# Strassen's scheme for the first product of batches 1 to 3 in an attention-and-FFN kernel, with a hand-written program order

## The chip, the cores and the metric

The kernel runs on one core of one Trainium2 chip. The metric is the device time of one execution in microseconds (us); below it is shown beside the span that the profiler recorded, which runs from the first to the last instruction. Engines are called by the profile's names: PE is TensorE's matmul and PEld its weight load, DVE is VectorE, ACT is ScalarE, POOL is GpSimd and SP issues the DMAs.

## The reference

For each of four batches, q, k and v are 6080 x 256. The columns of q and k are normalized, a 256 x 256 softmax is formed from them, and v is multiplied by it. The result goes through a two-layer network with an ELU in between.

```python
qn = q / (np.linalg.norm(q, axis=1, keepdims=True) + 1e-06)
kn = k / (np.linalg.norm(k, axis=1, keepdims=True) + 1e-06)
s = kn.transpose(0, 2, 1) @ qn / tau
a = softmax(s)                         # over the last axis, 256 x 256
x = (v @ a).reshape(24320, 256)
h = x @ w_in                           # 256 -> 2048
g = np.where(h > 0.0, h, np.exp(np.minimum(h, 0.0)) - 1.0)
out = g @ w_out                        # 2048 -> 256
```

## The kernel before

The softmax matrix is folded into the first weights: for each batch the kernel forms `wp` = a @ w_in (256 x 2048), so that h = v @ wp. Every large product runs in three matmuls instead of one: an operand is split into a part `hi` in the type fp32r and the remainder `lo`, and hi*hi, hi*lo and lo*hi are added up in PSUM (`split`, L113 to L115: a cast on ACT and a subtraction on DVE).

The 6080 positions of a batch are cut into 12 chunks of 512 or 496 columns (8 and 4 of them; `chunk_sizes`). One **step** is one chunk `c` and one block `f` of 128 of the 2048 hidden rows; there are 16 steps in a chunk and 768 in all. In a step, `h_item` (L417) runs six matmuls into a PSUM bank `ph` (two halves of 256 inputs, three terms each; L423 to L425). `elu` (L430) turns the bank into g: on even steps as ACT Exp (L438), DVE min and add (L439) and DVE max (L440), on odd steps as ACT Relu (L434), ACT Exp (L435) and one DVE instruction (L436). `split_g` (L443) casts g on ACT (L114) and takes the remainder on DVE (L115). Three steps later (`LAG`), `out_item` (L455) multiplies g by w_out, again with six matmuls (L461, L463, L465), into two banks that collect a chunk's output over 16 steps and are then copied by ACT (L487) and stored.

The order of the work is that of `take` (L833): step i emits the first product of step i, the split of step i-1 and the second product of step i-3. Beside it stand what the next batch needs, at step numbers that are written out in tables (`side`, `loose`, `fine`): loading q and k in 24 groups of rows, squaring them for the norms (L181, L182), splitting them and multiplying them into the Gram matrices (`gram_item`, L195; L203 and L210, 512 and 256 columns wide), then the norms and the softmax (L264 to L331), the transposes (L333), and `wp` itself (`wp_item`, L363). The matmuls of `fine` are threaded between those of `out_item`. Over batch 0's first four chunks the order on PE, DVE and ACT is the program's; from there on a scheduler places the instructions of the steps.

GpSimd does almost nothing: it clears a few tiles (L169). PSUM's eight banks are two for the Gram matrices, three for `ph` and what shares its tag `w`, and three for outputs (tag `o`).

## Time and profile before

| | |
|---|---|
| times of two runs | 2165.7 and 2166.98 us, median 2166.34 us |
| span of the profiled execution (no other time of it is given) | 2163.4 us |
| PE busy | 2158.6 us in 10240 recorded matmuls |
| DVE busy | 1527.0 us |
| ACT busy | 1469.1 us |
| POOL busy | 3.3 us in 11 instructions |
| DMA | 120.77 MB, 55 GB/s of HBM traffic over the span |

The time is the median of the runs without the profiler. The span is 2.9 us shorter than that median. Busy times are sums of recorded durations; the duration of an instruction on ACT or DVE runs until its result is written, and the next one may start a little earlier, so start times tell how densely instructions follow each other. A row of the timeline gives the start, the duration, the engine, the line, the operation, and the tiles with their shapes; in brackets stand an idle time ahead of it and what ended that.

### The profile page before, as it was taken

To read this page: it belongs to the slowest core of one execution; us is meant where nothing else is said; L and a number is where in the kernel's file an instruction comes from. 1 tells how busy PE (TensorE), PEld (TensorE's weight loads), DVE (VectorE), ACT (ScalarE), POOL (GpSimd) and SP (SyncE) were. 2 spreads that over 40 slices of the span, in tenths; PEclk is the share of its full clock that TensorE was granted. 3 is DMA by queue.
4 is the path that set the end of the run, shared out by engine and by line. 5 is a ranking of instruction groups with operands and counts; after the bars stand their busy time and mean duration, and the time that the engine had idled before them with its cause. 6 is when DMAs were issued, how large, how long until landed. Compare 5 with 4: busy or idle time off the path is not lost.

```text
span 2163.4 us, 27196 instructions
## 1 busy us (share of the span) xinstructions
PE 2158.6 (100%) x10240; PEld 1911.9 (88%) x10240; DVE 1527.0 (71%) x2358; ACT 1469.1 (68%) x2422; POOL 3.3 (0%) x11
## 2 busy tenths in 40 slices
PE   9999999999999999999999999999999999999999
PEld 8888888899888888889988888888998888888998
DVE  7987777778766776776776677667776666666665
ACT  6877777667666666666766666666776666666665
POOL 0000000000000000000000000000000000000000
PEclk9999999999999999999999999999999999999999
DMA  9320222221111111111111112111112000000000
GB/s 357 107 78 30 78 69 68 68 65 49 59 38 50 49 59 49 59 58 46 39 59 39 49 50 68 49 58 49 56 31 67 20 30 27 23 20 11 20 10 20
DMA packets 62532, 120.77 MB, mean 56 GB/s; under 512 B 6208, under 2 KB 16064, under 8 KB 62400
## 3 DMA queue, kind: packets, MB, share of 16 engines
q1 hardware_dynamic: 62256, 118.91, 16.6%
q8 instruction: 80, 1.31, 0.2%
q14 instruction: 52, 0.43, 0.1%
q10 hardware_dynamic: 144, 0.13, 0.0%
HBM read 92.01 MB, written 27.00 MB: 55 GB/s over the span
## 4 chain that ended last, share of the span: by engine, by line
PE 100%; ACT 0%; DVE 0%; issue 0%
PE po L465 15%; PE po L463 15%; PE ph L423 15%; PE po L461 15%; PE ph L424 15%; PE ph L425 15%; PE gram L203 3%; PE gram L549 2%; PE gram L210 1%; PE pw L374 1%; PE pw L373 1%; PE pw L375 1%; PE pe L549 0%; PE pw L370 0%; PE pd L222 0%; PE pt L337 0%
## 5 line engine op out<-in xcount | busy, mean ns | idle before, releaser
L114 ACT CAST g<-e 128x512 fp32r<-128x512 f32 (+1 forms) x768 | 469.6, 611 | 483.5 <-DVE e L440 281.6
L115 DVE TENSOR_TENSOR g<-e,g 128x512 fp32r<-128x512 f32 (+1 forms) x768 | 525.6, 685 | 323.0 <-ACT g L114 295.6
L465 PE MATMUL po<-g,wo 128*128 128x512 f32 (+1 forms) x1536 | 579.3, 377 | 0.0
L463 PE MATMUL po<-g,wo 128*128 128x512 f32 (+1 forms) x1536 | 579.2, 377 | 0.0
L461 PE MATMUL po<-g,wo 128*128 128x512 f32 (+1 forms) x1536 | 578.9, 377 | 0.0
L423 PE MATMUL ph<-vt,wp 128*128 128x512 f32 (+1 forms) x1472 | 555.4, 377 | 0.0
L425 PE MATMUL ph<-vt,wp 128*128 128x512 f32 (+1 forms) x1472 | 554.5, 377 | 0.0
L424 PE MATMUL ph<-vt,wp 128*128 128x512 f32 (+1 forms) x1472 | 554.5, 377 | 0.0
L436 DVE SCALAR_TENSOR_TENSOR e<-e,ph 128x512 f32<-128x512 f32 (+1 forms) x416 | 283.2, 681 | 242.5 <-ACT e L435 241.9
L434 ACT ACTIVATE e<-ph 128x512 f32<-128x512 f32 (+1 forms) x416 | 246.6, 593 | 129.1 <-PE ph L425 114.4
L461 PEld LDWEIGHTS po<-g,wo 128*128 128x128 f32 x1536 | 290.3, 189 | 37.9 <-DVE scr L478 0.2
L463 PEld LDWEIGHTS po<-g,wo 128*128 128x128 f32 x1536 | 290.3, 189 | 37.8
L465 PEld LDWEIGHTS po<-g,wo 128*128 128x128 f32 x1536 | 290.7, 189 | 34.8 <-DVE g L115 0.3
L424 PEld LDWEIGHTS ph<-vt,wp 128*128 128x128 f32 x1472 | 278.2, 189 | 36.2
L425 PEld LDWEIGHTS ph<-vt,wp 128*128 128x128 f32 x1472 | 278.2, 189 | 36.1
L423 PEld LDWEIGHTS ph<-vt,wp 128*128 128x128 f32 x1472 | 278.2, 189 | 36.1
L435 ACT ACTIVATE e<-e 128x512 f32<-128x512 f32 (+1 forms) x416 | 261.3, 628 | 12.6
L440 DVE TENSOR_TENSOR e<-ph,e 128x512 f32<-128x512 f32 (+1 forms) x352 | 240.6, 684 | 10.4
L438 ACT ACTIVATE e<-ph 128x512 f32<-128x512 f32 (+1 forms) x352 | 207.9, 591 | 31.1 <-PE ph L425 29.2
L439 DVE TENSOR_SCALAR e<-e 128x512 f32<-128x512 f32 (+1 forms) x352 | 147.0, 418 | 20.7 <-ACT e L438 20.6
L182 DVE TENSOR_TENSOR acc<-acc,sq 128x1024 f32<-128x1024 f32 x84 | 102.6, 1221 | 12.2 <-ACT sq L181 11.1
L203 PE MATMUL gram<-qk 128*128 128x512 f32 x268 | 101.6, 379 | 0.0
(134 smaller groups left out, 1183.1 us busy)
## 6 DMA issues: line engine op xcount, KB each, us to landing
raw<-in_q_dram SPq DMA_DIRECT2D x76, 256.0 KB, 2.7
raw<-in_k_dram SPq DMA_DIRECT2D x76, 256.0 KB, 3.0
v<-in_v_dram SPq DMA_DIRECT2D x32, 512.0 KB, 3.6
out_dram<-o SPq DMA_DIRECT2D x56, 256.0 KB, 2.1
v<-in_v_dram SPq DMA_DIRECT2D x16, 496.0 KB, 3.5
out_dram<-o SPq DMA_DIRECT2D x31, 248.0 KB, 2.1
wraw<-w_scr SPq DMA_DIRECT2D x12, 512.0 KB, 3.2
room<-in_q_dram SPq DMA_DIRECT2D x16, 256.0 KB, 5.2
```

The costliest lines, as they stand in the source:

```text
L114: nc.scalar.copy(hi, src)
L115: nc.vector.tensor_sub(lo, src, hi.bitcast(F32))
L423: nc.tensor.matmul(ph[:, 0:n], wp[kt][:, 0, fs], hi, start=(kt == 0), stop=False)
L424: nc.tensor.matmul(ph[:, 0:n], wp[kt][:, 0, fs], lo, start=False, stop=False)
L425: nc.tensor.matmul(ph[:, 0:n], wp[kt][:, 1, fs], hi, start=False, stop=(kt == KT - 1))
L434: nc.scalar.activation(ev, pv, AF.Relu, scale=-1.0)
L435: x = nc.scalar.activation(ev, ev, AF.Exp, scale=-1.0)
L436: y = nc.vector.scalar_tensor_tensor(ev, ev, -1.0, pv, op0=ALU.add, op1=ALU.max)
L440: y = nc.vector.tensor_tensor(ev, pv, ev, op=ALU.max)
L461: nc.tensor.matmul(o, wo[:, f, 0, ds], hi, start=first(c, f), stop=False)
L463: nc.tensor.matmul(o, wo[:, f, 1, ds], hi, start=False, stop=False)
L465: nc.tensor.matmul(o, wo[:, f, 0, ds], lo, start=False, stop=last(c, f))
```

## The change

Batch 0 stays as it was (some tiles share other buffers, and its first weights lie in another layout). From batch 1 on, a **unit** takes the place of four steps: one chunk `c` and one quarter `fq` (512) of the hidden rows. There are 144 units. In a unit, the 256 x 512 weights are cut into four blocks A11 to A22 (the first index names the half of the hidden rows, the second the half of the 256 inputs) and v's chunk into B11 to B22 (the second index names the half of the columns). Four sums of A-blocks (S1 to S4) and four of B-blocks (T1 to T4) are formed by GpSimd (`s_sum`, `t_sum`), split into hi and lo, and seven block products are made (`product`): A11 B11, S3 T3, S2 T2, A12 B21, S1 T1, S4 B22 and A22 T4. Each product is six matmuls of 256 (or 248) columns, so a unit has 42 of them; before, four steps had 24 of 512 (or 496) columns for the same h. The second product is as before, 24 matmuls to a unit (`multiply_out`).

Three PSUM banks hold the products. `bank_a` collects A11 B11 and A12 B21. `bank_b` is first filled by ACT with a copy of A11 B11, and then collects S2 T2, S1 T1 and S4 B22; ACT copies it out after the first (`u2`) and after the second (`u4`). `bank_e` collects S3 T3 and A22 T4; DVE adds it to `u4` after the first and to `u2` after the second. The four blocks of h are then `bank_a` (e11), `bank_b` at the end (e12), `u2` (e21) and `u4` (e22). All four go through Relu and Exp on ACT and one DVE instruction (`relu_exp`, `largest`). The cast to hi is made by DVE for e11 and e12 and by ACT for e22 and e21 (`hi_part`), the remainder by DVE (`lo_part`).

From the first unit on, the order on all engines is the program's. What the next batch and the next chunk need is put into lists with a cost for each task (`task`), and `spend` emits as many of them as a budget allows at fixed places of a unit: on ACT after the cast of e21 and after `u4`, on DVE ahead of `largest` of e11 and after the remainder of e11, on GpSimd in the same two places. `beside` threads the next batch's PE work between the second product's matmuls. GpSimd takes the sums, the casts of T and B blocks, and most of the additions of squares.

Three places of the new order matter below. In the rows, `s_0` to `s_3` are the tiles of A- and S-blocks, `t_0` and `t_1` those of T-blocks, `b_0` and `b_1` the two banks that units take in turn as `bank_b`, `held` is one tile that holds u2, e12 and e21, and `po` are the output banks.

The first is PE. One step of before (chunk 37, within batch 3):

```order
L423 MATMUL ph_14735<-vt_37_14461,wp_3_0_13661 128x512
L424 MATMUL ph_14735<-vt_37_14461,wp_3_0_13661 128x512
L425 MATMUL ph_14735<-vt_37_14461,wp_3_0_13661 128x512
L423 MATMUL ph_14735<-vt_37_14461,wp_3_1_13662 128x512
L424 MATMUL ph_14735<-vt_37_14461,wp_3_1_13662 128x512
L425 MATMUL ph_14735<-vt_37_14461,wp_3_1_13662 128x512
L461 MATMUL po_37_0_14667<-g_14706,wo_83 128x512
```

The start of a unit of the change (chunk 38, first quarter, batch 3):

```order
L1093 MATMUL bank_a_16953<-s_2_4967,s_0_4774 128x256 x6
L1093 MATMUL bank_e_16961<-t_0_4714,s_0_4774 128x256 x6
L1116 MATMUL po_37_0_16697<-g2_16844,wo_83 128x512
L1117 MATMUL po_37_0_16697<-g2_16844,wo_83 128x512
L1118 MATMUL po_37_0_16697<-g2_16844,wo_83 128x512
L1116 MATMUL po_37_1_16713<-g2_16844,wo_83 128x512
L1117 MATMUL po_37_1_16713<-g2_16844,wo_83 128x512
L1118 MATMUL po_37_1_16713<-g2_16844,wo_83 128x512
L1093 MATMUL b_0_5085<-t_0_4714,s_0_4774 128x256 x6
L1093 MATMUL bank_a_16953<-s_3_5093,s_0_4774 128x256 x6
L1116 MATMUL po_37_0_16697<-g1_16906,wo_83 128x512
```

Where a bank was filled once and read by the other engines, the banks are now read and filled again within the unit: the six matmuls into `b_0` (S2 T2) follow ACT's copy into that bank, and the six into `bank_a` (A12 B21) stand behind them on PE.

The second is ACT. Before, around the same place:

```order
L438 ACTIVATE e_14388<-ph_14381 128x512
L114 CAST g_14412<-e_14388 128x512
L434 ACTIVATE e_14408<-ph_14401 128x512
L435 ACTIVATE e_14408<-e_14408 128x512
L114 CAST g_14432<-e_14408 128x512
```

And ACT over the unit of the change, from the last two activations of the unit ahead (on e21) up to those on e21 of this one:

```order
L1176 ACTIVATE held_5089<-held_5089 128x512
L1455 COPY b_0_5085<-bank_a_16953 128x512
L1182 CAST g2_16943<-held_5089 128x2x256
L1468 COPY held_5089<-b_0_5085 128x512
L1175 ACTIVATE e_e11_5091<-bank_a_16953 128x512
L1176 ACTIVATE e_e11_5091<-e_e11_5091 128x512
L1476 COPY e_u4_5090<-b_0_5085 128x512
L1175 ACTIVATE e_e22_5092<-e_u4_5090 128x512
L1176 ACTIVATE e_e22_5092<-e_e22_5092 128x512
L1182 CAST g2_17038<-e_e22_5092 128x2x256
L1175 ACTIVATE held_5089<-b_0_5085 128x512
L1176 ACTIVATE held_5089<-held_5089 128x512
```

The copy that fills `b_0` for this unit (L1455) stands behind everything that ACT does for e22, e12 and e21 of the unit ahead, and three copies of PSUM banks (L1455, L1468, L1476) have come in.

The third is DVE over the same unit, from the remainders of the unit ahead to the remainder of e22:

```order
L1179 SCALAR_TENSOR_TENSOR held_5089<-held_5089 128x512
L1185 TENSOR_TENSOR g1_16906<-held_5089,g1_16906 128x2x256
L1185 TENSOR_TENSOR g2_16943<-held_5089,g2_16943 128x2x256
L1179 SCALAR_TENSOR_TENSOR e_e11_5091<-e_e11_5091,bank_a_16953 128x512
L1182 CAST g1_17003<-e_e11_5091 128x2x256
L1477 TENSOR_TENSOR e_u4_5090<-bank_e_16961,e_u4_5090 128x512
L1185 TENSOR_TENSOR g1_17003<-e_e11_5091,g1_17003 128x2x256
L1179 SCALAR_TENSOR_TENSOR e_e22_5092<-e_e22_5092,e_u4_5090 128x512
L1489 TENSOR_TENSOR held_5089<-bank_e_16961,held_5089 128x512
L1185 TENSOR_TENSOR g2_17038<-e_e22_5092,g2_17038 128x2x256
```

The addition that completes u4 (L1477), which ACT's work on e22 reads, stands behind DVE's work on e11 (L1179 and L1182).

The diff, cut to the new functions and the loop that sets the order:

```diff
--- before.py
+++ after.py
-    def split_g(c, e):
+    def split_g(c, e, i):
         n = span(c)[2]
-        g = work.tile([P, 2, CH], F32R, tag="g", bufs=4, name="g")
+        if i % 2 == 0:
+            state["g"] = work.tile([P, 2, 2, CH], F32R, tag="g", bufs=3, name="g")
+        g = state["g"][:, i % 2]
         split(g[:, 0, 0:n], g[:, 1, 0:n], e[:, 0:n])
         return g
...
@@ -746,7 +753,7 @@
     splits = [(1, 0, 0), (2, 4, 4), (3, 7, 9)]
-    splits += [(c, (c - 1) * FT + 9, (c - 1) * FT + 12) for c in range(M, NCH)]
+    splits += [(c, (c - 1) * FT + 9, (c - 1) * FT + 12) for c in range(M, NB)]
...
-    for b in range(1, B):
-        s0 = M * FT if b == 1 else chunk_of(b - 1) * FT + FT
...
+    HF = CH // 2
+    MATRICES = ("A11", "A22", "A12", "S1", "S2", "S3", "S4")
+    SPARE = len(MATRICES)
+
+    def new_s(fq):
+        s_tiles[fq] = work.tile([P, SPARE + 1, 2, HF], F32R, tag="wp", bufs=2 * KT, name=f"s_{fq}")
+
...
+    def s_scale(b, fq, ct):
+
+        if ct == 0:
+            new_x(b, fq)
+        pw = state.pop((b, "pw", fq, ct))
+        nc.scalar.activation(
+            x_of(b, fq, 2 * ct, 2 * ct + 2), halves_of_turns(pw), AF.Copy, scale=state[b, "rs"][:, ct : ct + 1]
+        )
+
+    def s_sum(b, fq, k):
+        a21, a11, a22, a12, s1, s2, s3, s4 = (x_of(b, fq, y, y + 1) for y in range(8))
+        add, sub = nc.gpsimd.tensor_add, nc.gpsimd.tensor_sub
+        (
+            lambda: add(s1, a21, a22),
+            lambda: sub(s2, s1, a11),
+            lambda: sub(s3, a11, a21),
+            lambda: sub(s4, a12, s2),
+        )[k]()
+
+    def s_hi(b, fq, lo, hi, copy=nc.scalar.copy):
+        copy(s_tiles[fq][:, lo:hi, 0], x_of(b, fq, 1 + lo, 1 + hi))
+
+    def s_lo(b, fq, lo, hi):
+        s = s_tiles[fq]
+        nc.vector.tensor_sub(s[:, lo:hi, 1], x_of(b, fq, 1 + lo, 1 + hi), s[:, lo:hi, 0].bitcast(F32))
+
+    s_tiles = {}
+    PARTS = ((0, 1), (1, 3), (3, 5), (5, SPARE))
+
+    b = 1
+    if True:
+        s0 = M * FT
         s1 = chunk_of(b) * FT
         length = s1 - FT - 14 - s0
...
@@ -860,8 +936,582 @@
     for i in range(M * FT + LAG):
         take(i)
     in_order.close()
-    for i in range(M * FT + LAG, len(steps) + LAG):
+
+
+    ACT, DVE, POOL, PE, SP, CAST, ADD = "act", "dve", "pool", "pe", "sp", "cast", "add"
+    queues = {(e, level): [] for e in (ACT, DVE, POOL, PE, SP, CAST, ADD) for level in range(4)}
+
...
+    def spend(engine, budget, now):
+        order = [(engine, 0), (engine, 1), *((x, y) for x in SHARED.get(engine, ()) for y in range(2)), (engine, 2), (engine, 3)]
+        for key in order:
+            queue = queues[key]
+            while queue and queue[0].ready(now, 0):
+                t = queue[0]
+                cost = t.cost if key[0] == engine else t.cost[engine]
+                if cost > budget:
+                    break
+                queue.pop(0)
+                budget -= cost
+                if key[0] == engine:
+                    t.fn()
+                else:
+                    t.fn({ACT: nc.scalar.copy, DVE: nc.vector, POOL: nc.gpsimd.tensor_copy if key[0] == CAST else nc.gpsimd}[engine])
+                t.done = now
+
...
+    PERIOD = 4
+    units = [(c, fq) for c in range(NB, NCH) for fq in range(FQ)]
+    begins = {c: PERIOD * FQ * (c - NB) for c in range(NB, NCH + 1)}
...
+    def t_sum(c, k):
+        hn = half_of(c)
+        if k == 0:
+            state["tt", c] = work.tile([P, 4, HF], F32, tag="raw", bufs=5, name=f"tt_{c}")
+        v = vraw[c]
+        b11, b12 = (v[:, 0, x * hn : (x + 1) * hn] for x in range(2))
+        b21, b22 = (v[:, 1, x * hn : (x + 1) * hn] for x in range(2))
+        t1, t3, t2, t4 = (state["tt", c][:, y, 0:hn] for y in range(4))
+        sub, add = nc.gpsimd.tensor_sub, nc.gpsimd.tensor_add
+        (
+            lambda: sub(t1, b12, b11),
+            lambda: sub(t3, b22, b12),
+            lambda: add(t2, t3, b11),
+            lambda: sub(t4, b21, t2),
+        )[k]()
+
+    def t_hi(c, k):
+        hn = half_of(c)
+        nc.gpsimd.tensor_copy(t_groups[c % 2][:, k : k + 2, 0, 0:hn], state["tt", c][:, k : k + 2, 0:hn])
+
+    def t_lo(c, k):
+        hn = half_of(c)
+        t = t_groups[c % 2][:, k : k + 2]
+        nc.vector.tensor_sub(t[:, :, 1, 0:hn], state["tt", c][:, k : k + 2, 0:hn], t[:, :, 0, 0:hn].bitcast(F32))
+        for y in range(2):
+            operands[c, TERMS[k + y]] = t[:, y]
+
+    TERMS = ("T1", "T3", "T2", "T4")
...
+    def b_hi(c, k):
+        to, src, hn, _ = block_of(c, k)
+        nc.gpsimd.tensor_copy(to[:, 0, 0:hn], src)
+
+    def b_lo(c, k):
+        to, src, hn, name = block_of(c, k)
+        nc.vector.tensor_sub(to[:, 1, 0:hn], src, to[:, 0, 0:hn].bitcast(F32))
+        operands[c, name] = to
...
+    def product(bank, c, fq, a, t, begin=False):
+        hn = half_of(c)
+        w, m = s_tiles[fq][:, MATRICES.index(a)], operands[c, t]
+        hi, lo = (in_turns(m[:, x, 0:hn]) for x in range(2))
+        for j in range(2):
+            js = slice(j * P, j * P + P)
+            for k, (x, y) in enumerate(((0, hi), (0, lo), (1, hi))):
+                nc.tensor.matmul(
+                    bank[:, j, 0:hn],
+                    w[:, x, js],
+                    y,
+                    start=(begin and j == 0 and k == 0),
+                    stop=(j == 1 and k == 2),
+                    skip_group_check=True,
+                )
...
+    def plan_chunk(c):
+
+        if c + 1 >= NCH:
+            return
+        d, t = c + 1, begins[c]
+        if c == NB:
+            task(SP, 0, lambda: new_t_group(d), when=t, level=0)
+        x = task(SP, 0, lambda: vraw.__setitem__(d, load_v(d)), when=t + PERIOD, level=0)
+        for k in range(4):
+            x = task(POOL, 0.65, lambda k=k: t_sum(d, k), [x], when=t + PERIOD, level=0)
+            if k % 2 == 1:
+                y = task(POOL, 0.65, lambda k=k: t_hi(d, k - 1), [x], when=t + PERIOD, level=0)
+                task(DVE, 0.685, lambda k=k: t_lo(d, k - 1), [y], when=t + PERIOD, level=0)
+        for k, when in enumerate((2 * PERIOD, 3 * PERIOD, 3 * PERIOD + 1)):
+            y = task(POOL, 0.35, lambda k=k: b_hi(d, k), [x], when=t + when, level=0)
+            task(DVE, 0.415, lambda k=k: b_lo(d, k), [y], level=0)
+
+    BOTH = {ACT: 0.61, POOL: 0.65}
+
...
+    for u, (c, fq) in enumerate(units):
+        now = PERIOD * u
+        b = c // NB
+        hn = half_of(c)
+        if fq == 0:
+            plan_chunk(c)
+        spend(SP, 1, now)
+        assert (b, fq) in s_ready, (b, fq, u)
+        e = {name: t[:, :, 0:hn] for name, t in e_tiles.items()}
+        bank_a = ps.tile([P, 2, HF], F32, tag="w", bufs=WB, name="bank_a")
+        product(bank_a, c, fq, "A11", "B11", True)
+        bank_b = banks_b[u % 2]
+        va, vb = bank_a[:, :, 0:hn], bank_b[:, :, 0:hn]
+        nc.scalar.copy(vb, va)
+        bank_e = ps.tile([P, 2, HF], F32, tag="w", bufs=WB, name="bank_e")
+        ve = bank_e[:, :, 0:hn]
+        product(bank_e, c, fq, "S3", "T3", True)
+        multiply_out(2, now)
+        if before is not None:
+            before()
+        spend(ACT, 1.9, now)
+        spend(POOL, 4.3, now)
+        spend(DVE, 2.5, now)
+        product(bank_b, c, fq, "S2", "T2")
+        product(bank_a, c, fq, "A12", "B21")
+        multiply_out(1, now)
+        nc.scalar.copy(e["u2"], vb)
+        product(bank_b, c, fq, "S1", "T1")
+        relu_exp(e["e11"], va)
+        largest(e["e11"], va)
+        g1 = work.tile([P, 2, 2, 2, HF], F32R, tag="g", bufs=3, name="g1")
+        hi_part(g1, 0, e["e11"], hn, nc.vector.tensor_copy)
+        spend(POOL, 1.3, now + 2)
+        multiply_out(2, now)
+        nc.scalar.copy(e["u4"], vb)
+        nc.vector.tensor_add(e["u4"], ve, e["u4"])
+        product(bank_b, c, fq, "S4", "B22")
+        spend(ACT, 1.25, now + 2)
+        lo_part(g1, 0, e["e11"], hn)
+        spend(DVE, 1.0, now + 2)
+        multiply_out(1, now)
+        product(bank_e, c, fq, "A22", "T4")
+        relu_exp(e["e22"], e["u4"])
+        largest(e["e22"], e["u4"])
+        multiply_out(2, now)
+        g2 = work.tile([P, 2, 2, 2, HF], F32R, tag="g", bufs=3, name="g2")
+        hi_part(g2, 1, e["e22"], hn, nc.scalar.copy)
+        nc.vector.tensor_add(e["u2"], ve, e["u2"])
+        relu_exp(e["e12"], vb)
+        relu_exp(e["e21"], e["u2"])
+        lo_part(g2, 1, e["e22"], hn)
+        largest(e["e12"], vb)
+        hi_part(g1, 1, e["e12"], hn, nc.vector.tensor_copy)
+
+        def before(e=e, g1=g1, g2=g2, hn=hn):
+            largest(e["e21"], e["u2"])
+            hi_part(g2, 0, e["e21"], hn, nc.scalar.copy)
+            lo_part(g1, 1, e["e12"], hn)
+            lo_part(g2, 0, e["e21"], hn)
+
+        for y, g in ((2, g1), (0, g2)):
+            for j in range(2):
+                for dt in range(DT):
+                    outs.append((c, 4 * fq + y + j, g[:, j], dt))
+
+    before()
+    now = PERIOD * len(units)
+    while outs:
+        multiply_out(1, now)
+        spend(ACT, 9, now)
+    for queue in queues.values():
+        assert not queue
+    in_order.close()
```

426 lines of the change are left out of this document (391 added, 35 removed).

## The prediction

> **What bounds the kernel now.** I read, in this order, the clock by core, the busy times, the chain that ended last, and the sums of a late window in which nothing is prepared for a next batch.
>
> ```profile
> core 0: 2163.4 us, clock 1.000
> PE 2158.6 (100%) x10240; PEld 1911.9 (88%) x10240; DVE 1527.0 (71%) x2358; ACT 1469.1 (68%) x2422; POOL 3.3 (0%) x11
> PE 100%; ACT 0%; DVE 0%; issue 0%
> 1700.00:2100.00 400.00, 400.00 (x1870) 353.10 (x1869) 250.75 (x408) 253.60 (x427) 0.00 (x0) 1.00 0.06 21
> ```
>
> PE works without a gap at a full clock, and the chain is PE alone; in the last row, 400 of 400 us. DVE and ACT are behind by 30% and nobody waits for them. So the time is the sum of what PE issues, and fewer columns shorten it as long as no other engine makes PE wait. The rate of issue comes from PE's and PEld's timelines:
>
> ```profile
> 1699.68 0.38 PE L423 MATMUL ph<-vt,wp 128*128 128x512 f32 x1
> ...
> 1703.99 0.38 PE L465 MATMUL po<-g,wo 128*128 128x512 f32 x1
> 1003.26 0.37 PE L423 MATMUL ph<-vt,wp 128*128 128x496 f32 x1
> 1003.47 0.37 PE L424 MATMUL ph<-vt,wp 128*128 128x496 f32 x1
> 1003.68 0.37 PE L425 MATMUL ph<-vt,wp 128*128 128x496 f32 x1
> 1004.52 0.27 PE L210 MATMUL gram<-qk 128*128 128x256 f32 x1
> 1004.63 0.38 PE L465 MATMUL po<-g,wo 128*128 128x496 f32 x1
> 519.29 0.53 PEld L278 LDWEIGHTS pn<-ones_r,acc_split 128*128 128x128 f32 x4
> 519.74 0.19 PEld L423 LDWEIGHTS ph<-vt,wp 128*128 128x128 f32 x1
> ```
>
> Between the first two rows lie 20 starts in 4.31 us: 0.2155 us for 512 columns; 0.21 for 496. A matmul of 256 columns lets the next start after 0.11 (1004.52 to 1004.63). Four weight loads with next to nothing to multiply between them follow each other every 0.1125 us (519.29 to 519.74), so a load hardly fits under 256 columns, and not at all under 248. I take 0.110 for both widths; the bounds are 0.106 (half of 0.21, for 248 columns) and 0.1125.
>
> **PE's own sum.** A unit had 48 matmuls: 10.34 us at 512 columns, 10.08 at 496. It now has 42 x 0.110 + 24 x 0.2155 = 9.79, or 42 x 0.110 + 24 x 0.21 = 9.66. That is 0.55 and 0.42 less, 0.51 on average over eight and four chunks, and 73 us over 144 units; with loads every 0.1125 us 58 us, with 0.109 and 0.106 for the two widths 85 us. This is the most that the change can bring, and it holds only where PE never waits.
>
> **The hand-offs.** In the new order PE waits for ACT and DVE inside a unit, where before three banks and three steps lay between them. Their paces come from their timelines, mostly with 496 columns (each row's start, then its duration):
>
> ```profile
> 1499.50 0.62 ACT L435 ACTIVATE e<-e 128x496 f32<-128x496 f32 x1
> 1004.09 0.58 ACT L438 ACTIVATE e<-ph 128x496 f32<-128x496 f32 x1
> 1515.25 0.58 ACT L434 ACTIVATE e<-ph 128x496 f32<-128x496 f32 x1
> 1515.87 0.62 ACT L435 ACTIVATE e<-e 128x496 f32<-128x496 f32 x1
> 1516.39 1.04 ACT L181 ACTIVATE sq<-raw 128x1024 f32<-128x1024 f32 x1
> 1518.28 0.58 ACT L438 ACTIVATE e<-ph 128x496 f32<-128x496 f32 x1
> 1518.75 0.60 ACT L114 CAST g<-e 128x496 fp32r<-128x496 f32 x1
> 1519.25 0.60 ACT L404 CAST vt<-v 128x496 fp32r<-128x496 f32 x1
> L487 ACT COPY o<-po 128x496 f32<-128x496 f32 x31 | 17.4, 573 | 3.2 <-PE po L465 2.4
> ```
>
> ```profile
> 1500.15 0.67 DVE L436 SCALAR_TENSOR_TENSOR e<-e,ph 128x496 f32<-128x496 f32 x1 [0.68 <-ACT e L435]
> 1503.37 0.41 DVE L439 TENSOR_SCALAR e<-e 128x496 f32<-128x496 f32 x1
> 1503.70 0.67 DVE L115 TENSOR_TENSOR g<-e,g 128x496 fp32r<-128x496 f32 x1
> 1504.29 0.67 DVE L440 TENSOR_TENSOR e<-ph,e 128x496 f32<-128x496 f32 x1
> 1513.36 0.42 DVE L439 TENSOR_SCALAR e<-e 128x496 f32<-128x496 f32 x1 [0.44 <-ACT e L438]
> 1513.82 0.67 DVE L440 TENSOR_TENSOR e<-ph,e 128x496 f32<-128x496 f32 x1
> ```
>
> Relu to its own Exp takes 0.62 (1515.25 to 1515.87), Exp to the next instruction 0.52, a cast 0.50, a copy out of PSUM 0.47 to 0.50 (read from L438). Across engines the whole duration counts and 0.03 more: Exp at 1499.50 ends at 1500.12, DVE begins at 1500.15. ACT begins 0.04 after the matmul's recorded end (1003.68 + 0.37 to 1004.09). On DVE a step takes 0.59, and an instruction that reads the one ahead of it begins 0.04 after that one's end (1513.36 + 0.42 to 1513.82). The casts that DVE gets are not in the trace; the nearest row is L439, also one tensor in SBUF, after which the next begins 0.33 later; the other end is L115 with 0.59. I take 0.33.
>
> Now one round, with time 0 where PE has issued S2 T2 and A12 B21 and goes on. A result of 256 columns stands 0.27 - 0.11 = 0.16 later and ACT begins at 0.20: Relu and Exp of e11 end at 1.44. DVE: `largest` 1.47 to 2.14, its cast begins at 2.18, the addition to u4 at 2.51 and ends at 3.18. ACT: Relu and Exp of e22, 3.21 to 4.45. DVE: `largest`, ends at 5.15. ACT: cast of e22 from 5.18, e12 from 5.68, e21 from 6.82, and at 7.96 the copy into `bank_b`, which ends at 8.53. PE begins S2 T2 of the next unit at 8.57, and its twelve matmuls end at 9.89. With 512 columns some twelve durations are 0.015 to 0.02 longer: 10.09. So this round is **longer than PE's own 9.66 and 9.79**. PE should stand still for some 0.2 to 0.3 us before S2 T2, in every unit that has nothing else to fill it; behind S2 T2 on PE stands A12 B21, for which ACT's e11 waits, so the delay goes round and is not made up. What remains of the gain there is 10.08 - 9.89 = 0.19 and 10.34 - 10.09 = 0.25.
>
> **Output copies.** In one unit of four ACT copies a chunk's two output banks between the cast of e21 and the copy of u2. In the round, Exp of e21 is written 1.83 before time 0 and DVE's `largest` ends at -1.13; the cast runs from -1.10 to -0.60, two copies of 0.48 to 0.36, that of u2 to 0.84. Relu of e11 should begin at 0.20, so the round is 0.65 longer. Four units: 4 x 10.09 + 0.65 = 41.0 against 41.4, and 40.2 against 40.3: 0.27 us saved on average.
>
> **Units with Gram work.** In 48 of the 144 units, eight Gram matmuls stand between the second product's: four of 512 and four of 256 columns, 1.30 us, as much as before. Only PE's own time grows by it, to 11.0; the round stays near 10.0, and ACT's four or five more instructions of about 0.5 fit into the rest. There PE is the bound and the whole 0.51 is saved: **24 us**. The other 96 units are 24 groups of four: **6 us**.
>
> **What is added.** The norms and softmax of batches 2 and 3 now stand in ACT's and DVE's fixed order, within units that have no reserve.
>
> ```profile
> L226 ACT ACT_TABLE_LOAD x4 | 5.1, 1283 | 0.1
> L230 ACT ACT_TABLE_LOAD x4 | 5.1, 1283 | 0.1
> L234 DVE RECIPROCAL ry<-ry 128x260 f32<-128x260 f32 x3 | 5.3, 1779 | 0.1
> L169 POOL MEMSET raw<- 128x512 f32 x3 | 2.1, 715 | 1516.7 <-DVE qk L115 1516.7
> ```
>
> The square root brings two table loads, 2.6 us and some 0.5 for the two activations, where ACT had 0.8 us free: 2.4 us late, twice, 5 us. DVE gets three to seven more instructions in about 16 such units (reciprocals in halves of 0.9 us, remainders of 0.6) and has 2 us free ahead of `largest` of e11; 0.6 us late each is 9 us (0 if they slip into waits, 20 if each is a whole instruction late). The last unit has no later work over its e21, and the first starts with empty queues: 4 us. Loads and stores stay as many as they were; they are now issued in program order, a unit or more ahead, on DMA engines that are 6% busy in the window above: nothing.
>
> **The sum** is made against the span of 2163.4 us: -24 - 6 + 5 + 9 + 4 = -12, so 2151.4; the median of the runs lies 2.9 above the span, so **2154 us**.
>
> **Rivals.** *PE stays the bound everywhere.* It needs a round shorter by 0.3 us, or less late work than I count. For it speaks that both ACT and DVE have 30% of their time free; against it, that free time cannot be moved along a chain in program order. Time: 2163.4 - 73 + 2.9 = 2093, from 2081 to 2108 by the bounds of the issue rate.
>
> *GpSimd and DVE get in each other's way.* GpSimd goes from 11 instructions to some 450, all in SBUF. The trace shows no GpSimd work beside DVE's but three memsets, so it excludes nothing. If a DVE instruction with two tensors in SBUF, or the cast, waited for a GpSimd instruction, the price would be at least the memset's 0.73 us. With Gram work GpSimd has about two additions a unit and DVE three remainders beside them: two waits, 1.46 against 1.0 us of reserve, some 0.4 x 48 = 19 us. Without it, nine GpSimd instructions fall on four units, and the cast of e11 and `largest` of e22 lie on the round: at most 0.73 x 96 = 70 us, and at 0.44 a unit 42. Time: 2154 + 19 + 42 = 2215, slower; the upper end is 2243. It decides from 0.39 us lost per unit on. The Trainium skill, SBUF — State Buffer, section "SBUF: two separate sides", states just this: the two engines share a pair of ports, held as an exclusive lock for a whole instruction; no run so far shows it. The Trainium skill, GPSIMD Engine Reference, section "Elementwise — side-by-side cycle accounting", gives 2.6 cycles per element for two inputs, an estimate of 1.1 us for 512; by that the 19 us would be some 58.
>
> That the seven products are not seven is excluded: the order of the build has 42 matmuls of 256 columns per unit.
>
> **How the numbers follow.** My forecast, a round of hand-offs that takes back most of PE's gain, gets 0.52; PE as the bound 0.27; GpSimd in the way 0.21. A measurement of this kernel can tell about 2% from no change, 2123 and 2210 us. The forecast's own range, 2120 to 2195, lies nearly all between; 0.04 of it falls below and 0.02 above. The first rival is faster, but for 0.01; four fifths of the second are slower. So: faster 0.30, same 0.51, slower 0.19. The range of 8 in 10 takes in most of both rivals: 2088 to 2222 us.
>
> **What would show it.** Right: PE busy some 96 to 98% of the span; in batch 3 PE idle before L1093, released by ACT's copy L1455, 0.2 to 0.3 us in most units; units of 10.0 to 10.1 us there and of 11.0 with Gram work. Wrong: hardly any idle time on PE (the first rival); or DVE durations far above 0.69 us while POOL is at work (the second); or a spacing of the 256-column matmuls outside 0.106 to 0.1125, which moves every term.

## The result, and the profile after

The changed kernel takes **2257.84 us** (median of two runs, 2257.54 to 2258.13) against 2166.34: a ratio of 1.0424, 95% interval 1.0394 to 1.0454. It is 4% slower, and 104 us above the forecast.

Its page, the clock and the late window that answers to the one shown of the kernel before:

```profile
core 0: 2255.8 us, clock 0.999
PE 2157.1 (96%) x12834; PEld 1929.0 (86%) x12834; DVE 1845.6 (82%) x2802; ACT 1674.6 (74%) x2912; POOL 418.5 (19%) x487
PE 37%; ACT 31%; DVE 25%; issue 6%; POOL 0%; DMA 0%; ACTq 0%; SPq 0%; DVEq 0%; POOLq 0%
1700.00:2100.00 400.00, 382.12 (x2450) 340.24 (x2451) 318.15 (x506) 292.61 (x509) 71.80 (x97) 1.00 0.08 27
```

The chain was PE alone; now PE has 37% of it, and ACT and DVE have 56%. In the late window PE works 382 of 400 us. Note POOL: 0% of the chain, though 78 us will turn out to hang on its work. The chain names who was released by whom, and hardly anybody waits for POOL by a semaphore.

What PE waits for, in its two largest groups that wait (last column: idle time, and who ended it):

```profile
L1093 PE MATMUL b<-t,s 128*128 128x256 f32 (+1 forms) x1728 | 255.3, 284 | 46.7 <-ACT b L1455 29.5 <-ACT held L1468 14.2
L1093 PE MATMUL bank_e<-t,s 128*128 128x256 f32 (+1 forms) x1728 | 247.6, 280 | 44.6 <-DVE e_u L1477 29.2 <-DVE held L1489 13.2 <-DVE e L441 1.6
```

The wait for ACT's copy (L1455) was foreseen. The wait for DVE's addition to u4 (L1477) is as long, and wasn't.

The unit lengths tell where. I take a unit as the time from one start of ACT's copy into `bank_b` (L1455) to the next. Without Gram work (512 columns, units 100 to 127) four in a row take on average 10.32, 10.89, 10.32 and 11.17 us: 42.70, against 4 x 10.34 = 41.4 before and a forecast of 41.0. With Gram work (units 8 to 24 and 52 to 73) they take on average 13.81, 11.44, 12.62 and 11.84: 49.71, against 4 x 11.64 = 46.6 before (10.34 and 1.30 for the Gram matmuls) and a forecast of 4 x 11.0 = 44.0.

**The plain unit.** ACT, then DVE, then PE, in one unit of 10.33 us in which GpSimd does nothing:

```profile
1823.96 0.58 ACT L1455 COPY b<-bank_a 128x512 f32<-128x512 f32 x1
1826.23 0.60 ACT L1175 ACTIVATE e_e<-bank_a 128x512 f32<-128x512 f32 x1
1829.31 0.63 ACT L1175 ACTIVATE e_e<-e_u 128x512 f32<-128x512 f32 x1 [1.17 <-DVE e_u L1477]
1831.41 0.62 ACT L1182 CAST g<-e_e 128x512 fp32r<-128x512 f32 x1 [0.82 <-DVE e_e L1179]
1834.29 0.58 ACT L1455 COPY b<-bank_a 128x512 f32<-128x512 f32 x1
```

```profile
1827.52 0.69 DVE L1179 SCALAR_TENSOR_TENSOR e_e<-e_e,bank_a 128x512 f32<-128x512 f32 x1 [1.37 <-PE b L1093]
1828.25 0.43 DVE L1182 CAST g<-e_e 128x512 fp32r<-128x512 f32 x1
1828.59 0.68 DVE L1477 TENSOR_TENSOR e_u<-bank_e,e_u 128x512 f32<-128x512 f32 x1
1830.63 0.69 DVE L1179 SCALAR_TENSOR_TENSOR e_e<-e_e,e_u 128x512 f32<-128x512 f32 x1 [0.76 <-ACT e_e L1176]
```

```profile
1834.92 0.94 PE L1093 MATMUL b<-t,s 128*128 128x256 f32 x6 [0.19 <-ACT b L1455]
1835.69 0.83 PE L1093 MATMUL bank_a<-s,s 128*128 128x256 f32 x6
1836.36 0.42 PE L1116 MATMUL po<-g,wo 128*128 128x512 f32 x1
```

This is the forecast's round, step for step, down to PE's 0.19 us of idle time. From Relu of e11 to the copy it takes 8.06 us (1826.23 to 1834.29), where I had 7.76 with 496 columns and some 0.15 to 0.2 more with 512. The cast's row begins at 1828.25 and the next at 1828.59: 0.34 us for DVE's cast, where I had chosen 0.33.

**A unit with Gram work.** POOL and DVE in the unit of 13.98 us that begins at 743.92:

```profile
746.00 2.96 POOL L1278 TENSOR_TENSOR acc<-acc,sq 128x512 f32<-128x512 f32 x2 [8.50 <-ACT sq L1274]
748.92 1.19 POOL L1018 TENSOR_TENSOR tt<-v 128x256 f32<-128x256 f32 x1
```

```profile
746.03 3.48 DVE L1295 TENSOR_TENSOR qk<-raw,qk 128x512 fp32r<-128x512 f32 x2
749.44 0.67 DVE L1179 SCALAR_TENSOR_TENSOR e_e<-e_e,bank_a 128x512 f32<-128x512 f32 x1
750.15 0.93 DVE L1182 CAST g<-e_e 128x512 fp32r<-128x512 f32 x1
751.60 1.18 DVE L1185 TENSOR_TENSOR g<-e_e,g 128x512 fp32r<-128x512 f32 x1
```

Two remainders of 0.69 us take 3.48 us while GpSimd makes two additions; `largest` of e11 starts where the second of them ends. The cast takes 0.93 instead of 0.43. But `largest`, which reads a bank of PSUM, takes its usual 0.67 us, with a GpSimd instruction across it. The groups of DVE say the same over the whole kernel (after the bar: busy time, then mean ns):

```profile
L1295 DVE TENSOR_TENSOR qk<-raw,qk 128x512 fp32r<-128x512 f32 x96 | 108.9, 1160 | 0.0
L1051 DVE TENSOR_TENSOR s<-v,s 128x256 fp32r<-128x256 f32 (+1 forms) x108 | 79.2, 733 | 0.0
L1182 DVE CAST g<-e_e 128x512 fp32r<-128x512 f32 (+1 forms) x144 | 74.3, 516 | 4.9
L1179 DVE SCALAR_TENSOR_TENSOR e_e<-e_e,e_u 128x512 f32<-128x512 f32 (+1 forms) x144 | 112.2, 779 | 57.4 <-ACT e_e L1176 56.7
L1179 DVE SCALAR_TENSOR_TENSOR e_e<-e_e,bank_a 128x512 f32<-128x512 f32 (+1 forms) x144 | 97.7, 679 | 96.6 <-ACT e_e L1176 49.0 <-PE b L1093 47.3
L1477 DVE TENSOR_TENSOR e_u<-bank_e,e_u 128x512 f32<-128x512 f32 (+1 forms) x144 | 97.5, 677 | 0.8 <-ACT e_u L1476 0.8
```

The last two read PSUM and have their usual mean. The first four have all operands in SBUF, and all are stretched. Two theories went to the chip. **C** (contention): GpSimd's instructions hold up those of DVE. **O** (order): the fixed order, with ACT's and DVE's added tasks in it, is too long by itself. Both may hold.

### The profile page after: what moved, and what is told of

Its sections match the earlier page's. It is cut to its first block, busy times and chain, and to the rows that moved or that the text cites. A ratio compares the mean times of both kernels' runs of the same rounds, so it can differ in the third digit from the quotient of the medians.

```text
span 2255.8 us, 33898 instructions
## 1 busy us (share of the span) xinstructions
PE 2157.1 (96%) x12834; PEld 1929.0 (86%) x12834; DVE 1845.6 (82%) x2802; ACT 1674.6 (74%) x2912; POOL 418.5 (19%) x487
## 4 chain that ended last, share of the span: by engine, by line
PE 37%; ACT 31%; DVE 25%; issue 6%; POOL 0%; DMA 0%; ACTq 0%; SPq 0%; DVEq 0%; POOLq 0%
DVE e_e L1179 8%; ACT held L1176 7%; ACT held L1175 6%; ACT g L1182 5%; PE b L1093 4%; ACT e_e L1176 4%; ACT e_e L1175 4%; PE ph L428 3%; PE ph L429 3%; PE ph L430 3%; PE po L472 3%; PE po L470 3%; PE po L468 3%; DVE g L1182 3%; DVE e_u L1477 3%
## 5 line engine op out<-in xcount | busy, mean ns | idle before, releaser
L1116 PE MATMUL po<-g,wo 128*128 128x512 f32 (+1 forms) x1158 | 440.9, 381 | 1.0 <-DVE g L1182 1.0
L1118 PE MATMUL po<-g,wo 128*128 128x512 f32 (+1 forms) x1158 | 437.7, 378 | 0.7 <-DVE g L1185 0.6
L1117 PE MATMUL po<-g,wo 128*128 128x512 f32 (+1 forms) x1158 | 437.4, 378 | 0.0
L1093 PEld LDWEIGHTS b<-t,s 128*128 128x128 f32 x1728 | 222.6, 192 | 104.3 <-ACT b L1455 61.2
L1093 PE MATMUL b<-t,s 128*128 128x256 f32 (+1 forms) x1728 | 255.3, 284 | 46.7 <-ACT b L1455 29.5
L1093 PE MATMUL bank_e<-t,s 128*128 128x256 f32 (+1 forms) x1728 | 247.6, 280 | 44.6 <-DVE e_u L1477 29.2
L1093 PEld LDWEIGHTS bank_e<-t,s 128*128 128x128 f32 x1728 | 223.4, 191 | 70.8 <-DVE e_u L1477 44.0
L1118 PEld LDWEIGHTS po<-g,wo 128*128 128x128 f32 x1158 | 219.2, 189 | 30.0 <-DVE g L1185 2.2
L1117 PEld LDWEIGHTS po<-g,wo 128*128 128x128 f32 x1158 | 220.9, 191 | 13.9
L1116 PEld LDWEIGHTS po<-g,wo 128*128 128x128 f32 x1158 | 221.3, 191 | 12.0 <-DVE g L1182 1.4
L1185 DVE TENSOR_TENSOR g<-e_e,g 128x512 fp32r<-128x512 f32 (+1 forms) x288 | 206.4, 717 | 19.6
L1185 DVE TENSOR_TENSOR g<-held,g 128x512 fp32r<-128x512 f32 (+1 forms) x288 | 201.5, 701 | 11.7
L1182 ACT CAST g<-e_e 128x512 fp32r<-128x512 f32 (+1 forms) x144 | 88.5, 615 | 141.2 <-DVE e_e L1179 139.5
L1179 DVE SCALAR_TENSOR_TENSOR e_e<-e_e,bank_a 128x512 f32<-128x512 f32 (+1 forms) x144 | 97.7, 679 | 96.6 <-ACT e_e L1176 49.0
L115 DVE TENSOR_TENSOR g<-e,g 128x512 fp32r<-128x512 f32 (+1 forms) x192 | 131.8, 686 | 48.8 <-ACT g L114 47.5
L114 ACT CAST g<-e 128x512 fp32r<-128x512 f32 (+1 forms) x192 | 116.7, 608 | 71.0 <-DVE e L445 38.4
```

Source lines behind the costliest of these rows:

```text
L114: nc.scalar.copy(hi, src)
L115: nc.vector.tensor_sub(lo, src, hi.bitcast(F32))
L1093: nc.tensor.matmul(bank[:, j, 0:hn], w[:, x, js], y, start=(begin and j == 0 and k == 0), stop=(j == 1 and k == 2), skip_group_check=True,)
L1116: yield nc.tensor.matmul(o, wo[:, f, 0, ds], hi, start=begin, stop=False)
L1117: yield nc.tensor.matmul(o, wo[:, f, 1, ds], hi, start=False, stop=False)
L1118: yield nc.tensor.matmul(o, wo[:, f, 0, ds], lo, start=False, stop=end)
```

## The experiments

All edits are made to the changed kernel. "Plain four" and "Gram four" are the sums of four units as above; ratios are to the kernel before, timed beside each run.

| run | us | ratio, 95% interval | plain four | Gram four |
|---|---|---|---|---|
| the change | 2257.8 | 1.0424 (1.0394 to 1.0454) | 42.70 | 49.71 |
| r1, GpSimd's work left out | 2180.1 | 1.0069 (1.0054 to 1.0084) | 41.88 | 44.76 |
| r2, only its additions left out | 2211.9 | 1.0215 (1.0200 to 1.0230) | 42.73 | 45.49 |
| r3, e22's cast late | 2167.5 | 1.0008 (0.9998 to 1.0017) | 39.69 | 46.85 |
| r5, u4 first | 2221.4 | 1.0257 (1.0240 to 1.0274) | 41.56 | 48.30 |
| r6, r3 and r5 together | 2153.4 | 0.9941 (0.9927 to 0.9956) | 39.83 | 45.78 |
| r7, r6 with GpSimd's work left out | 2120.8 | 0.9792 (0.9777 to 0.9807) | 39.48 | 44.62 |
| r8, all of g cast by ACT | 2399.8 | 1.1081 (1.1062 to 1.1099) | 46.74 | 53.82 |
| r9, r6 with DVE in GpSimd's place | 2160.3 | 0.9975 (0.9966 to 0.9985) | 40.23 | 44.96 |
| r12, r9 spread out | 2149.4 | 0.9925 (0.9911 to 0.9940) | 39.48 | 45.74 |
| r13, r12 with tasks ahead of e11 | 2148.0 | 0.9919 (0.9904 to 0.9934) | 39.48 | 44.97 |
| r15, r13 only in Gram units | 2139.3 | 0.9882 (0.9865 to 0.9898) | 39.48 | 44.96 |

**GpSimd's work taken away (r1, r2).** In r2 the one line of the squares; in r1 also, from the third chunk on, the sums and casts (DVE's remainder then reads v in place of the sum, so that it stays):

```
 def add(engine, y=y):
+    if engine is nc.gpsimd:
+        return
...
 def t_sum(c, k):          # t_hi and b_hi likewise
+    if c >= NB + 2:
+        return
```

> From the third chunk of batch 1 on, GpSimd's sums, casts of the T operands and of the B blocks, and from the start its additions of squares are left out (stale operands and short norms, so the output is not the reference's); every instruction of ACT, DVE and PE stays. Theory C (DVE instructions with all operands in SBUF stand behind GpSimd's): the four kinds of Gram unit, 11.4, 12.6, 12.0 and 14.0 us, all become 11.0 to 11.4, and every fourth unit without Gram work falls from 11.18 to 10.32; that is 12 x 4.4 + 24 x 0.86 = 73 us, so 2185 us. Theory O (the order alone is too tight: ACT's and DVE's added tasks stand in the round, GpSimd disturbs nobody): no change, 2258 us, and L1295 keeps its 1.16 us mean.

> Only GpSimd's 71 additions of squares are left out (the norms come out short); its work for the chunks stays. Theory C: Gram units of 12.6 and 12.0 us fall to about 11.4, those of 14.0 to some 12.8; 12 x 3 = 36 us, so 2222 us; units without Gram work stay. Theory O: 2258 us.

Measured: 2180.1 and 2211.9 us, 78 and 46 us less than the change (73 and 36 were expected). The groups of DVE in r1, and its window over Gram units:

```profile
L1304 DVE TENSOR_TENSOR qk<-raw,qk 128x512 fp32r<-128x512 f32 x96 | 63.4, 687 | 0.0
L1058 DVE TENSOR_TENSOR s<-v,s 128x256 fp32r<-128x256 f32 (+1 forms) x108 | 48.3, 447 | 0.0
L1189 DVE CAST g<-e_e 128x512 fp32r<-128x512 f32 (+1 forms) x144 | 61.1, 424 | 4.9
743.92:793.92 50.00, 50.00 (x332) 46.61 (x331) 41.75 (x70) 42.98 (x78) 0.00 (x0) 1.00 0.20 64
```

The remainders are back from 1160 to 687 ns with the same instructions on DVE. In the window over Gram units PE works 50 of 50 us: with GpSimd at rest the order is no bound there. The units of 11.18 us without Gram work became 10.32; those of 10.32 and 10.89 stayed. Theory O alone is out. But r1 is still 0.7% slower than the kernel before, so C is not everything: four plain units take 41.88 us, where the kernel before needed 41.4.

**The round made shorter (r3, r5).** In r3 ACT no longer waits in the round for DVE's `largest` of e22. The cast of e22 moves behind the copy into `bank_b` (L1455), where the cast of e21 stood from the start; that copy stands behind all else that ACT does for the unit ahead, but not behind that cast:

```
-hi_part(g2, 1, e["e22"], hn, nc.scalar.copy)     # ahead of Relu of e12
...
 def before(e=e, g1=g1, g2=g2, hn=hn):
+    hi_part(g2, 1, e["e22"], hn, nc.scalar.copy)
     largest(e["e21"], e["u2"])
...
+    lo_part(g2, 1, e["e22"], hn)
```

In r5 DVE's `hi_part(g1, 0, e["e11"], ...)` moves behind `tensor_add(e["u4"], ve, e["u4"])`.

> The cast of e22 (ACT) and its remainder (DVE) move behind the copy into bank_b, so that ACT no longer waits in the round for DVE's largest of e22. If the round of hand-offs holds the plain units at 10.32 us, it is now some 1.2 us shorter and PE's own 9.8 us take over: plain units 9.8 to 9.9, the unit with output copies about 9.9 instead of 10.88, Gram units 0.4 to 1.0 us shorter; in all about 90 to 110 us, 2150 to 2170. If another chain (DVE's own order, or ACT's total) is right behind, plain units stay above 10.1 and the gain is under 40 us. If GpSimd's disturbance sits in parts that the shorter round does not cover, the units of 11.18 and 14.0 stay more than 1 us above their neighbours.

> DVE adds to u4 before it casts e11, so the cast (0.35 to 0.43 us) leaves the round. If the round bounds the plain units, they fall from 10.32 to 9.95 us, those with output copies from 10.88 to 10.5; 96 x 0.35 = 34 us and up to 17 us in Gram units, so 2207 to 2225 us. If PE or ACT's total bounds them, no change: 2258 us.

Measured: 2167.5 and 2221.4 us, as expected (r3 by 90, r5 by 36 us). Two windows of r3, Gram units and plain ones:

```profile
743.92:793.92 50.00, 47.85 (x314) 43.69 (x313) 47.39 (x67) 40.46 (x73) 19.26 (x20) 1.00 0.20 64
1900.00:2000.00 100.00, 100.00 (x668) 93.28 (x668) 79.66 (x135) 78.19 (x136) 18.69 (x27) 1.00 0.07 22
```

One cast, moved, and PE works 100 of 100 us in plain units, GpSimd's work included: the shorter round has room for it. In Gram units PE still idles 2 of 50 us. So a part of O holds as well: the round did bound the plain units.

**Both shortenings, with and without GpSimd's work (r6, r7).**

> Both shortenings of the round together: e22's cast behind the copy into bank_b, and the addition to u4 ahead of e11's cast. GpSimd as in the change. Theory C+O (the round, and GpSimd's disturbance on top): with e22's cast late, plain units already run at PE's rate, so only what GpSimd stretches can still gain; 0 to 12 us better than 2167.5, so 2155 to 2167. If the round alone were the cause, it would now be shorter than PE's own time everywhere, and the time would fall to about 2110.

> Both shortenings, and GpSimd's work for the chunks and its additions of squares left out (stale operands, short norms; not the reference's output). Theory C+O: PE is the bound nearly everywhere, four plain units take 39.2 to 39.4 us, Gram units 11.0 to 11.1, and 12 x 2.9 + 24 x 0.6 us and more fall away from the 2167 of the late cast: 2100 to 2125 us. If something else (ACT's or DVE's total, PE's restarts) holds the units, the time stays above 2140.

Measured: 2153.4 us, some 2 us better than its range, and 2120.8 us, within its range. The same two windows of r7:

```profile
743.92:793.92 50.00, 50.00 (x333) 46.69 (x333) 40.93 (x70) 43.38 (x79) 0.00 (x0) 1.00 0.23 75
1900.00:2000.00 100.00, 100.00 (x673) 93.98 (x672) 77.67 (x136) 78.36 (x136) 0.00 (x0) 1.00 0.07 22
```

PE is the bound in both: this is its own sum at last. Even in the shorter round GpSimd costs 2153.4 - 2120.8 = 33 us; in the order of the change it cost 78. The two causes overlap, and their prices do not add up: the shorter round alone is worth 104 us (r6), GpSimd at rest alone 78 (r1), and both together 137 (r7). r6 computes all of the reference and is 0.6% faster than the kernel before (0.4 to 0.7% by its interval).

**The other half of the change undone (r8).** Both `hi_part(g1, ..., nc.vector.tensor_copy)` become `nc.scalar.copy`.

> The change with one part undone: ACT casts all of g, as before; DVE casts none. Worked out on the round: u4's copy waits behind e11's cast, which waits for DVE's largest, and e12's cast stands ahead of the copy into bank_b: plain units 11.1 to 11.2 us instead of 10.32, Gram units some 0.5 us longer, so 2340 to 2370 us. If the halves do not matter, because ACT has a quarter of its time free: 2258 us or less, since DVE then loses two casts that GpSimd can hold up.

Measured: 2399.8 us; the direction is right, and the size short by 30 us: plain units are 11.64 us, where I had 11.15 (the granted clock was 0.988, against 0.999 in the changed kernel). ACT's wait for DVE's `largest`, in the changed kernel and then in r8 (total, times, longest):

```profile
ACT g L1182 <- DVE e_e L1179: 139.5, 142, 2.0
```

```profile
ACT g L1182 <- DVE e_e L1179: 283.0, 285, 2.8
```

Now ACT waits twice in a round for `largest`, once for e11 and once for e22, about 1 us each. Without casts on DVE the scheme would lose 142 us more: that half of the change was a help.

**GpSimd's work added at chosen places (r10, r11, r14).** One more GpSimd addition in each of the last 44 units; the three runs differ in what it reads, and so in when it is ready:

```
+if u >= 100:
+    nc.gpsimd.tensor_add(held[:, 3, :, 0:hn], held[:, 3, :, 0:hn], e["e11"])
 hi_part(g1, 0, e["e11"], hn, nc.vector.tensor_copy)      # r10; r11: behind it, reading the cast; r14: behind lo_part
```

> The change, with one more GpSimd addition of 512 columns in each of the last 44 units (on a spare tile, result unused), which becomes ready when DVE's largest of e11 is done and so meets DVE's cast of e11. Theory C (a DVE instruction whose operands all lie in SBUF waits until GpSimd's instruction has ended): the cast takes 1.4 to 1.5 us instead of 0.43, it lies on the round, and each of the 44 units is 1.0 to 1.1 us longer: 2258 + 46 = 2304 us. Theory O (no disturbance): 2258 us, the cast stays at 0.43 us.

> The same additional GpSimd work, ready one DVE instruction later: it meets DVE's addition to u4, which reads PSUM, and then the remainder of e11 in SBUF, which has about 1 us to spare in the round. If only instructions with all operands in SBUF wait: the addition to u4 keeps its 0.68 us, the remainder takes 1.2 to 1.4 us, and the time stays at 2258 us (up to 2268). If any DVE instruction waits for GpSimd: the addition to u4 takes 1.7 us or more, and the time is about 2304 us as in the run beside it.

Measured: 2264.4 and 2269.3 us (1.0454, 1.0437 to 1.0472, and 1.0478, 1.0462 to 1.0493). **My expectation for r10 failed**: 7 us, not 46. r11 is 1 us above the 2268 that its first theory allowed. DVE and POOL in a unit of r10:

```profile
1840.38 0.43 DVE L1183 CAST g<-e_e 128x512 fp32r<-128x512 f32 x1
1840.72 0.68 DVE L1480 TENSOR_TENSOR e_u<-bank_e,e_u 128x512 f32<-128x512 f32 x1
1841.32 1.18 DVE L1186 TENSOR_TENSOR g<-e_e,g 128x512 fp32r<-128x512 f32 x1
```

```profile
1840.42 1.52 POOL L1475 TENSOR_TENSOR held<-held,e_e 128x512 f32<-128x512 f32 x1 [4.62 <-DVE e_e L1180]
```

The cast was 0.04 us ahead, so it kept its 0.43 us and GpSimd's addition waited (1.52 instead of 1.28 us). The addition to u4, which reads PSUM, keeps 0.68 in the midst of it. The remainder of e11 then waits until GpSimd ends (1840.42 + 1.52 = 1841.94) and ends 0.56 later; it lies beside the round. So whoever comes first goes first. In r11 a unit without other GpSimd work takes 10.34 us, 0.02 more than without the addition, though others grew because GpSimd's work for the chunk was pushed to a worse place (11.68 instead of 10.89). One collision on the round was still to be shown:

> The change, with one more GpSimd addition of 512 columns in each of the last 44 units, ready when DVE has written the remainder of e11, some 0.6 us before DVE's largest of e22, which has all its operands in SBUF and lies on the round. Theory C: GpSimd is first, largest of e22 takes about 1.25 us instead of 0.69, and plain units without other GpSimd work are 10.9 us instead of 10.32; 44 x 0.5 to 0.6 us, so 2280 to 2286 us. If collisions cost nothing on the round (the whole loss was the order): 2258 us, the units stay at 10.32.

Measured: 2278.4 us (1.0519, 1.0503 to 1.0534), 2 us short of the range of theory C. POOL and DVE:

```profile
1853.53 1.28 POOL L1483 TENSOR_TENSOR held<-held,g 128x512 f32<-128x512 f32 x1 [8.79 <-DVE g L1186]
```

```profile
1854.15 1.21 DVE L1180 SCALAR_TENSOR_TENSOR e_e<-e_e,e_u 128x512 f32<-128x512 f32 x1 [0.76 <-ACT e_e L1177]
```

GpSimd runs until 1854.81, and `largest` ends 0.55 us after that, at 1855.36 instead of 1854.84. The unit without other GpSimd work is 10.87 us, 0.55 more than 10.32. The same addition costs 0.02 us at one place and 0.55 at another: this is theory C, measured by itself.

**GpSimd's work given to DVE (r9, r12, r13, r15).** All four have both shortenings and compute all of the reference; GpSimd keeps only the sums of the softmax stage, some of its casts and a few small things (68.6 us busy in r15, 418.5 in the change).

```
-SHARED = {ACT: (CAST,), DVE: (ADD,), POOL: (CAST, ADD)}
+SHARED = {ACT: (CAST,), DVE: (ADD,), POOL: (CAST,)}
...
-            x = task(POOL, 0.65, lambda k=k: t_sum(d, k), [x], when=t + PERIOD, level=0)
+            x = task(DVE, 0.415, lambda k=k: t_sum(d, k), [x], when=t + PERIOD, level=0)      # r12 on: when=t + PERIOD * (1 + k // 2)
...
-        spend(DVE, 2.5, now)
+        spend(DVE, 3.9, now)      # r12: 2.8, r13: 4.3, r15: 4.3 if u % 48 < 27 else 2.8
```

> Both shortenings, and GpSimd's work for the chunks and the additions of squares given to DVE (whole computation). Theory C+O: no DVE instruction waits, plain units stay at PE's rate, and DVE's own total sets the Gram units: 7.0 us of the round, two remainders, two additions and 0.8 us for the chunk are some 11.0 to 11.5 us against PE's 11.0; 2110 to 2145 us, 1 to 2.5% faster than before the change. If DVE's total costs as much as the disturbance did, Gram units stay near 12 us and the time near 2160.

> As the run with both shortenings and DVE in GpSimd's place, but the sums and casts of a chunk's T operands lie in two units instead of one (eight DVE instructions in one unit made every fourth plain unit 11.5 us, and four of them 40.24 us against PE's 39.5), and DVE's budgets are 2.8 and 1.4 us. If the burst was the loss: four plain units take 39.5 to 39.7 us, and the time is 2130 to 2150 us. If DVE's total sets it: 2155 to 2165 us.

> The same, with budgets of 4.3 and 0.7 us, so that nearly all of DVE's added tasks stand ahead of largest of e11, where it has up to 1.7 us idle in plain units, and hardly any ahead of largest of e22. If the place ahead of largest of e22 costs more: 5 to 15 us better than the run beside it; if a full budget ahead of e11 makes Gram units late: 5 to 15 us worse.

> As the run with budgets of 4.3 and 0.7 us, but these hold only in the 27 units of a batch that have Gram work; in the others DVE takes 2.8 and 1.0 us. If bursts of DVE tasks in the softmax units are what is left against the run with GpSimd's work left out: units of 13 to 15 us disappear, and the time is 2130 to 2140 us. If it is DVE's total or another wait: 2145 to 2150 us.

Measured: 2160.3, 2149.4, 2148.0 and 2139.3 us. r9 missed its range: its Gram units are as short as expected (44.96 for four), but every fourth plain unit took 11.5 us with eight of the chunk's instructions in one. Its neighbours were shorter, so four units lost 40.23 - 39.48 = 0.75 us. Spread over two units (r12), plain units run at PE's rate; by the two traces this gave 8 us there and 8 in the softmax units, and took 6 in the Gram units. r13 gained neither the 5 to 15 us nor lost them: its Gram four is 0.77 shorter than r12's, but its softmax stage has five units of 13 to 15 us, where r12 has two, and r15, with one left, gets 9 us back. Two windows of r15:

```profile
743.92:793.92 50.00, 50.00 (x332) 46.65 (x332) 47.77 (x88) 43.26 (x79) 0.00 (x0) 1.00 0.23 75
1900.00:2000.00 100.00, 100.00 (x672) 93.73 (x671) 86.91 (x161) 79.77 (x139) 0.00 (x0) 1.00 0.10 32
```

DVE is busy 48 of 50 us in Gram units, yet PE never waits there. So DVE can carry GpSimd's work when it is handed out well: with it r9 is 7 us slower than r6, and r15 is 14 us faster. r6 with r15's budgets was not run, so how much of the 14 us the budgets give by themselves is not shown. **r15 is 1.2% faster than the kernel before** (1.0 to 1.4% by its interval). What separates it from r7 (18.5 us) lies mostly in the softmax stage: 15 us by the two traces (units there go up to 13.9 us, in r7 up to 12.5). That was not tried further.

## Why the prediction was wrong

- **The step that failed** is in the forecast's Gram units: "ACT's four or five more instructions of about 0.5 fit into the rest. There PE is the bound and the whole 0.51 is saved". That holds with GpSimd at rest: r1 has 44.76 us for four of them, and PE works through its window. The step costed DVE's instructions at 0.59 to 0.69 us though GpSimd worked beside them, and the sum put GpSimd's price at nothing. Measured: (49.71 - 44.76) / 4 x 48 = 59 us in the Gram units and (42.70 - 41.88) x 24 = 20 in the others, 79 together; r1 shows 78 as a whole. These two are scaled up from a few units; added up unit by unit, the traces have 54 us in the Gram units and 22 in the others, 14 of them in the softmax units.
- **The second rival was the right mechanism**, and I gave it 0.21. Its sign, its place and the rows to look for were right. Its price was wrong in both parts, with the errors in opposite directions: 19 us with Gram work (59 measured) and 42 us without (20), 61 where 78 were measured. (Its own 1.46 - 1.0 is 0.46, which makes 22 us, not 19.) The waiting time was bounded from a memset of 0.73 us, where an addition of 512 columns takes 1.28 alone and a 0.69 us remainder beside it up to 1.8; and I set 1.0 us of reserve against it, which GpSimd's two additions and the chunk's sums used up. So of the 43 us between its 2215 and the 2258 measured, 17 are its own price, and 26 are what the forecast under it lacked: r1, with GpSimd's work left out, takes 2180.1 and not 2154. The Trainium skill, SBUF — State Buffer, section "SBUF: two separate sides", says that of a DVE instruction with two SBUF inputs or in a two-port mode and a GpSimd instruction, the one that starts first has the shared ports for its whole length; r10 (DVE first) and r14 (GpSimd first) agree with it, and so does the PSUM-reading row of 0.68 us. The estimate of 1.1 us from the Trainium skill, GPSIMD Engine Reference, section "Elementwise — side-by-side cycle accounting", was nearer to the addition's 1.28 us than my bound by the memset, and so were the 58 us that it made of the 19. In part that was luck: r2 puts the additions alone at (49.71 - 45.49) x 12 = 51 us, and the rest of the 59 belongs to the sums and casts for the chunks.
- **The round of hand-offs** was right in kind: PE idle 0.19 us before S2 T2, released by L1455, as forecast (0.2 to 0.3). PE's share of the span, 96%, also came out as forecast, though the time did not: it could not tell the forecast from the second rival, while the lengths of the units could. In size the round was 10.33, not 10.09, and 10.13, not 9.89. Half of the 0.24 is on PE: after the wait the first six matmuls take 0.77 us (1834.92 to 1835.69) and the next six 0.67 (to 1836.36), where six by 0.110 are 0.66. The rest is Relu out of SBUF (1829.31 to 1829.97, 0.66 before its Exp begins) and ACT's start after `largest` (0.09, not 0.03). Output copies: 0.56, forecast 0.65. Over 24 fours: (41.88 - 41.0) x 24 = 21 us that the forecast lacked.
- **PE's own sum**: r7's plain unit of 9.87 us makes (9.87 - 24 x 0.2155) / 42 = 0.112 us per matmul of 256 columns, and 9.71 makes 0.111 at 248, within my bounds of 0.106 to 0.1125 and near the end set by the loads. A Gram unit is 44.62 / 4 = 11.16, not 11.0. But the 11.0 did not fit the forecast's own sum: all Gram units lie in chunks of 512 columns, for which 9.79 + 1.30 is 11.09, and the 0.51 that was counted as saved leaves 11.64 - 0.51 = 11.13. Against this r7 lacks 0.03 x 48 = 1 us, and r1, with 44.76 / 4 = 11.19, lacks 3.
- **Added work and ends**: 79 + 21 + 3 is 103, and 104 were lost, so the 18 us for table loads, softmax tasks and ends came out about right in sum. Their parts were not separated, and with terms scaled up from a few units a match this close is partly luck.
- **The first rival** (PE the bound everywhere, 2093, from 2081 to 2108) came nearest with both shortenings and GpSimd's work left out: r7, 2120.8. Of the 28 us between, (0.07 + 0.08 + 0.05) x 48 = 10 are the issue rate (Gram units 11.16 against 11.09, plain ones 9.87 against 9.79 and 9.71 against 9.66); the other 18 are left for the softmax stage and the ends, for which it had nothing.

## What to carry to other kernels

An engine that is off the chain, and for which hardly anyone waits, can still be the largest cost that a forecast lacks: before work is moved to GpSimd, count which DVE instructions beside it have all operands in SBUF, and price each at up to a whole GpSimd instruction, most of all where the order is fixed and full. Where a round of hand-offs bounds a unit, look for an instruction in it that waits and for which nobody waits, such as e22's cast: moving that one was worth 90 us, more than the 73 us that the scheme was to save on PE. Part of it is room for GpSimd's delays, for the shorter round brings their price down from 78 to 33 us. And hand tasks to a fixed order in pieces over several units; eight in one unit cost 0.75 us in every four (40.23 against 39.48).

## What the runs showed of the hardware that was not expected

- DVE and GpSimd take turns by whole instructions, and the first one goes: 0.04 us decided in r10 who waited. Both lose; GpSimd's additions of squares have a mean of 1426 ns in the changed kernel and 1.28 us alone.
- A DVE instruction with one operand in PSUM isn't touched: 677 to 683 ns on average in the kernel with GpSimd's work and in r1. Of the changed kernel's 144 additions to u4 (L1477) none took more than 687 ns.
- PE loses some 0.10 us more than its idle time at a wait: the next six matmuls of 256 columns take 0.77 us instead of 0.67 (medians in the changed kernel, 130 sixes of the products behind an idle time and 517 others).
